# Attention and two MLPs in one kernel: transposed weights in one-bank buffers, sums in SBUF, gate after both products, another choice of engines

## The chip, the cores and the metric

The kernel runs on one core of a Trainium2 chip. The metric is the device time of one execution in microseconds (us). A core has TensorE (PE, matrix products, with a queue of weight loads shown as PEld), VectorE (DVE), ScalarE (ACT), GpSimd (POOL) and SyncE (SP, which here only issues transfers). PSUM, where PE writes, has eight banks, each of which holds 512 fp32 numbers per partition.

## The reference

```python
# q, k, v: 2 batches, 12 heads, 448 rows, 64 columns, fp32
scores = where(upper triangle, -1e9, q @ k.T / 8)
attn = exp(scores - rowmax);  attn = attn / (rowsum + 1e-9)
x = (attn @ v), heads side by side                    # 896 x 768
xn = x / sqrt(mean(x * x) + 1e-6) * rms_g
g = xn @ w_gate;  h = g * sigmoid(g) * (xn @ w_val)    # 768 -> 1536
x = h @ w_out                                         # 1536 -> 768
h = max(x @ moe2_w_in, 0);  out = (h * h) @ moe2_w_out # 768 -> 2048 -> 768
```

The MLP weights arrive as 64-bit floats, two 32-bit words each.

## The kernel before

Attention goes by pairs of heads: 2 batches with 6 pairs, 12 in all, each `step(p)`. Scores of a pair are written in two PSUM tiles of two banks (`s1`, `s2`, pool `ps_s`, two buffers: four banks). DVE takes row maxima (L368, L370), ACT turns them into biases (`nb`, L375) and computes exp with `accum_out` (L395), which leaves the row sums in `su`. `su` is a slice of one PSUM tile, `sums_`, a bank of its own that all pairs share (four slices in turn). DVE adds 1e-9 and inverts (L410, L411), and POOL multiplies the seven pieces of exponentials by the result (`ml`, L421). PE transposes them with an identity: `tr1` (L436) once per head for `p1`, and `tr2`, `tr3` (L442, L446) for `p2`, all into tiles of two banks from a pool with one buffer (`ps_t`). Four copies (`c_1` to `c_4`, by ACT or DVE through `copy`, L282) bring a pair's 2,048 columns into `pt`, and `values` (L485) multiplies them with v: four chunks for each of two heads, 16 matmuls into `o`. `finish` copies `o` to `xr`, and `square` and `add_square` (L507 to L512) sum squares for the normalisation. The last PSUM bank, `ps_o`, holds `o`.

Beside that, six weight tiles of the first MLP are made ready (`ahead_steps`): from the two words of each double come an exponent part (L179, L181), a sign (L187, L191), upper and lower bits (L195, L200), and a split into an upper part (L158) and a lower rest (L208). `norm` scales x of a batch (L567) and splits it the same way (L158, L160, L578). `ahead_products` then computes the first three column tiles of the first MLP for the first batch: 18 matmuls for the gate's product and 18 for the other (L647), in the two banks of one `ps_s` tile, with tanh (L658), the gate (L662) and the final product (`hh`, L669).

All of these steps go to one planner, `Order`. Each step has a due time, the engines that may do it with a duration each in us, the steps that it follows and the buffers that it takes. The planner repeatedly picks the step that can begin first, within SLACK by due time, and gives it the engine where begin + duration + COST is least. Steps are emitted in that order, so it fixes each engine's queue; on the chip each queue runs in order and waits for what it needs. `A_`, `D_`, `P_` and `E_` are the durations that the planner assumes for ACT, DVE, POOL and PE.

After the planned part, `mlp1` runs the same three column tiles for the second batch and then the remaining nine for both (`mm3`, L227 to L229), followed by the products with `w_out`, `moe2_w_in` and `moe2_w_out`. There the order is that of the program.

Of the kernel before, what the change touches and what calls it, by code (L numbers as in the profile page):

```python
# [8 lines left out]
F32 = mybir.dt.float32  # L9
# [9 lines left out]
P = 128  # L19
# [4 lines left out]
NF2 = DF2 // P  # L24
NPAIR = H // 2
WARM = 9
ACC = 0.16
CN = 112
NE = 3
STRIDE = 6.0  # L30
SLACK = 0.1
SWITCH = 0.18
COST = {"D": 0.6}
LAT = {"E": 0.3, "S": 0.0}


# [7 lines left out]
class Order:  # L44
# [9 lines left out]
    def add(self, due, opts, f, after=(), new=(), uses=(), mode=None, begin=0.0):  # L54

        t = dict(due=due, opts=opts, f=f, after=[a for a in after if a], new=new, uses=list(uses) + list(new),
                 mode=mode, begin=begin, end=None, eng=None, i=len(self.tasks))
        for b in t["uses"]:
            b.left += 1
        self.tasks.append(t)  # L60
        return t
# [55 lines left out]
def tile_attention_moe_moe2(ctx: ExitStack, tc: tile.TileContext, qk, v, wg, wv, wo, w2i, w2o, rms_g, out):  # L117
# [122 lines left out]
    at = att.enter_context(tc.tile_pool(name="at", bufs=2))  # L240
    atc = att.enter_context(tc.tile_pool(name="atc", bufs=1))
    ps_s = att.enter_context(tc.tile_pool(name="ps_s", bufs=2, space=PSUM))
    ps_t = att.enter_context(tc.tile_pool(name="ps_t", bufs=1, space=PSUM))
    ps_o = att.enter_context(tc.tile_pool(name="ps_o", bufs=1, space=PSUM))
    ps_n = att.enter_context(tc.tile_pool(name="ps_n", bufs=1, space=PSUM))
    sums_ = ps_n.tile([P, 512], F32, name="sums_")

    NPR = B * NPAIR
    SC = 1.0 / float(D) ** 0.5
# [20 lines left out]
    for i in range(2):  # L270
# [1 line left out]
        nc.gpsimd.memset(t[:, 1, S:], 0.0)  # L272
        p2t.append(t)
    L3 = 1408
    KO = (0, S, 896, 1344)

    order = Order(dict(qk=3, v=NV, s=2, p1=2, p2=2, t=1, pt=2, o=1, x=9, sq=1, ssq=1, rb=1, raw=2, wt=3, whl=3,
                       early=3, tt=2, tu=2, hh=2))
    BOTH = (slice(0, D), slice(D, P))

    def copy(e, o, i):
        (nc.scalar.copy if e == "A" else nc.vector.tensor_copy)(o, i)  # L282
# [5 lines left out]
        return 0.15 + n / 960  # L288

    def P_(n, two=False):  # L290
        return 0.14 + 0.0024 * n if two else 0.27 + 0.00108 * n

    def E_(n):
        return n / 600 + 0.05
# [7 lines left out]
    def step(p):  # L302
# [2 lines left out]
        T0 = p * STRIDE  # L305
        add = order.add
        bq, bv, b1, b2, bp1, bp2 = (order.buf(n) for n in ("qk", "v", "s", "s", "p1", "p2"))
        bt1, bt2, bpt, bo, bx = (order.buf(n) for n in ("t", "t", "pt", "o", "x"))

        def load_qk(e):  # L310
            z["qk"] = at.tile([P, 2, S], F32, tag="qk", name="qk", bufs=3)
# [47 lines left out]
        def mx(buf, o, n, k):  # L359
            def f(e):  # L360
                if k == 0:
                    z["mx"] = at.tile([P, 8], F32, tag="mx", name="mx", bufs=3)
                    z["nb"] = at.tile([P, 8], F32, tag="nb", name="nb", bufs=3)
                    z["su"] = sums_[:, 8 * (p % 4):8 * (p % 4 + 1)]
                    z["r"] = at.tile([P, 8], F32, tag="r", name="r", bufs=3)
                src = z[buf][:, :, o:o + n]
                if k == 6:
                    nc.vector.tensor_reduce(z["mx"][:, 6:7], src, mybir.AxisListType.XY, ALU.max)  # L368
                else:
                    nc.vector.tensor_reduce(z["mx"][:, k:k + 2], src, AX, ALU.max)  # L370
            return f
# [55 lines left out]
                           uses=[bp1 if k < 4 else bp2]))  # L427


        def tr1(h):  # L430
            def f(e):
                if h == 0:
                    z["t1"] = ps_t.tile([P, 2, 512], F32, tag="t", name="t1")
                for i, o in enumerate((0, 128, 256, 384)):

                    nc.tensor.transpose(z["t1"][:, h, o:o + P], z["p1"][:, h, o:o + P], ident)  # L436
            return f

        def tr2(e):
            z["t2"] = ps_t.tile([P, 2, 512], F32, tag="t", name="t2")  # L440
            for i in range(4):
                nc.tensor.transpose(z["t2"][:, 0, i * P:(i + 1) * P], z["p2"][:, 0, i * P:(i + 1) * P], ident)  # L442

        def tr3(e):
            for i in range(4):
                nc.tensor.transpose(z["t2"][:, 1, i * P:(i + 1) * P], z["p2"][:, 1, i * P:(i + 1) * P], ident)  # L446

        a1 = add(T0 + 7, {"E": 0.44}, tr1(0), [ml_[0], ml_[2]], new=[bt1], uses=[bp1], mode="f")
        a2 = add(T0 + 7, {"E": 0.44}, tr1(1), [ml_[1], ml_[3], a1], uses=[bt1, bp1], mode="f")
        a3 = add(T0 + 10, {"E": 0.44}, tr2, [ml_[4], ml_[5]], new=[bt2], uses=[bp2], mode="f")  # L450
        a4 = add(T0 + 10, {"E": 0.44}, tr3, [ml_[6], a3], uses=[bt2, bp2], mode="f")


        def c_1(e):
            z["pt"] = at.tile([P, 2, L3], F32, tag="pt", name="pt", bufs=2)
            copy(e, z["pt"][:, :, 0:128], z["t1"][:, :, 0:128])

        def c_2(e):
            copy(e, z["pt"][:, :, 256:256 + 3 * 320].rearrange("p h (k n) -> p h k n", n=320)[:, :, :, :128],
                 z["t1"][:, :, 128:].rearrange("p h (k n) -> p h k n", n=128))  # L460

        def c_3(e):

            copy(e, z["pt"][:, :, 128:128 + 2 * 320].rearrange("p h (k n) -> p h k n", n=320)[:, :, :, :128],
                 z["t2"][:, 0].rearrange("p (h k n) -> p h k n", h=2, n=128))

        def c_4(e):

            copy(e, z["pt"][:, :, 128:].rearrange("p h (k n) -> p h k n", n=320)[:, :, :, 256:],
                 z["t2"][:, 1].rearrange("p (k h n) -> p h k n", h=2, n=D))  # L470

        def c2opt(n):
            return {"A": A_(n), "D": D_(n)}

        y1 = add(T0 + 8, c2opt(256), c_1, [a1, a2], new=[bpt], uses=[bt1])
        y2 = add(T0 + 8, c2opt(768), c_2, [a1, a2, y1], uses=[bt1, bpt])
        y3 = add(T0 + 11, c2opt(512), c_3, [a3, y1], uses=[bt2, bpt])
        y4 = add(T0 + 11, c2opt(512), c_4, [a4, y1], uses=[bt2, bpt])

        def values(e):  # L480
            z["o"] = ps_o.tile([P, 512], F32, tag="o", name="o")
            for j in range(4):
                n = S - j * P
                for h in range(2):
                    nc.tensor.matmul(z["o"][BOTH[h], j * P:S], z["v"][:, j, h * D:(h + 1) * D],  # L485
                                     z["pt"][:, h, KO[j]:KO[j] + n], start=j == 0, stop=j == 3)

        va = add(T0 + 13, {"E": E_(1024) + 0.15}, values, [t_v, y1, y2, y3, y4], new=[bo], uses=[bpt, bv], mode="c")

        def finish(e):  # L490
            z["x"] = xrp.tile([P, S], F32, tag="xr", name="xr")
# [143 lines left out]
    def ahead_products(ft, due):  # L635

        z, add = {}, order.add
        bs, bt, bu, bh = order.buf("s"), order.buf("tt"), order.buf("tu"), order.buf("hh")
        last = None

        def products(k, i):
            def f(e):
                if k == 0 and i == 0:
                    z["ps"] = ps_s.tile([P, 2, 512], F32, tag="s", name="pgv")
                o, w, x = z["ps"][:, k, :S], ahead[2 * ft + k]["hl"], xs[0][i]
                for n, (a_, b_) in enumerate(((0, 0), (0, 1), (1, 0))):
                    nc.tensor.matmul(o, w[:, a_, i], x[:, b_], start=i == 0 and n == 0, stop=i == NCC - 1 and n == 2)  # L647
            return f

        for k in range(2):  # L650
            for i in range(NCC):
                new = [bs] if k == 0 and i == 0 else []
                last = add(due, {"E": 0.61}, products(k, i), [last, xl[0][i], ahead[2 * ft + k]["done"]],
                           new=new, uses=[ahead[2 * ft + k]["bw"]] + ([] if new else [bs]), mode="f")
            if k == 0:
                def f_tanh(e):
                    z["t"] = tmp.tile([P, S], F32, tag="t", name="t")
                    nc.scalar.activation(z["t"], z["ps"][:, 0, :S], AF.Tanh, scale=0.5)  # L658

                def f_gate(e):  # L660
                    z["w"] = tmp.tile([P, S], F32, tag="u", name="u")
                    nc.vector.scalar_tensor_tensor(z["w"], z["t"], 1.0, z["ps"][:, 0, :S], ALU.add, ALU.mult)  # L662

                g1 = add(due, {"A": A_(S)}, f_tanh, [last], new=[bt], uses=[bs])
                g2 = add(due, {"D": D_(S)}, f_gate, [g1], new=[bu], uses=[bs, bt])

        def f_hh(e):
            z["hh"] = tmp.tile([P, S], F32, tag="hh", name="hh")
            nc.vector.scalar_tensor_tensor(z["hh"], z["w"], 0.5, z["ps"][:, 1, :S], ALU.mult, ALU.mult)  # L669

        def f_hi(e):
            hs[0][ft] = slab(f"h0_{ft}", 0, ft)
            rnd(E(e), hs[0][ft][:, 0], z["hh"])

        def f_lo(e):
            E(e).tensor_sub(hs[0][ft][:, 1], z["hh"], hs[0][ft][:, 0].bitcast(F32))

        g3 = add(due, {"D": D_(S)}, f_hh, [g2, last], new=[bh], uses=[bs, bu])
        g4 = add(due, {"A": A_(S), "P": P_(S)}, f_hi, [g3], uses=[bh])
        add(due, {"P": P_(S, True), "D": D_(S)}, f_lo, [g4], uses=[bh])  # L680
# [120 lines left out]
```

## Time and profile before

| | us |
|---|---|
| median of three runs | 624.02 |
| lowest, highest | 622.49, 626.37 |
| the profiled execution | 624.11 |
| its span, from the first to the last instruction | 622.2 |

| engine | busy in the span |
|---|---|
| PE | 599.8 |
| PEld | 524.7 |
| DVE | 408.8 |
| POOL | 262.9 |
| ACT | 129.0 |

Busy times are averages over very different stretches: up to about 105 us all engines work on attention, the six weight tiles and the first normalisation; up to about 140 us PE finishes attention and the products that were taken ahead; from there to the end PE multiplies without a break. Matmuls are pipelined, so PE's busy time says that it had work and not that it worked at its peak. A wait is put down to whichever releaser came last.

### The profile page before, as it was taken

To read this page: it belongs to the slowest core of one execution; us is meant where nothing else is said; L and a number is where in the kernel's file an instruction comes from. 1 tells how busy PE (TensorE), PEld (TensorE's weight loads), DVE (VectorE), ACT (ScalarE), POOL (GpSimd) and SP (SyncE) were. 2 spreads that over 40 slices of the span, in tenths; PEclk is the share of its full clock that TensorE was granted. 3 is DMA by queue.
4 is the path that set the end of the run, shared out by engine and by line. 5 is a ranking of instruction groups with operands and counts; after the bars stand their busy time and mean duration, and the time that the engine had idled before them with its cause. 6 is when DMAs were issued, how large, how long until landed. Compare 5 with 4: busy or idle time off the path is not lost.

```text
span 622.2 us, 8412 instructions
## 1 busy us (share of the span) xinstructions
PE 599.8 (96%) x3269; PEld 524.7 (84%) x3269; DVE 408.8 (66%) x570; ACT 129.0 (21%) x341; POOL 262.9 (42%) x318
## 2 busy tenths in 40 slices
PE   7998888989999999999999999999999999999997
PEld 4665555869999999999999999999999999999996
DVE  3689798165888777777755555888888874544310
ACT  4886666331000000000010001111111100000000
POOL 4559899333433333333322222566554442222100
PEclk9999898998999999999999999999999999999999
DMA  6454521001524333333333333233333234433100
GB/s 162 140 150 173 186 72 61 2 1 55 176 80 146 114 117 121 108 102 101 111 124 121 102 102 103 101 102 102 106 108 103 82 117 158 131 104 133 44 29 31
DMA packets 19496, 65.04 MB, mean 105 GB/s; under 512 B 2048, under 2 KB 8960, under 8 KB 19456
## 3 DMA queue, kind: packets, MB, share of 16 engines
q1 hardware_dynamic: 19456, 64.50, 31.9%
q8 instruction: 26, 0.43, 0.3%
q14 instruction: 14, 0.11, 0.1%
HBM read 61.74 MB, written 2.75 MB: 104 GB/s over the span
## 4 chain that ended last, share of the span: by engine, by line
PE 87%; POOL 6%; DVE 3%; ACT 2%; issue 1%; DMA 1%; SPq 0%; POOLq 0%; ACTq 0%; DVEq 0%
PE py L228 17%; PE py L229 17%; PE py L227 17%; PE pg L227 4%; PE pg L228 4%; PE pg L229 4%; PE pv L228 4%; PE pv L229 4%; PE pv L227 4%; PE pgv L647 4%; POOL p2t L421 2%; PE s L334 2%; POOL p L421 2%; PE o L485 2%; DVE mx L370 1%
## 5 line engine op out<-in xcount | busy, mean ns | idle before, releaser
L158 POOL TENSOR_SCALAR whl<-wt 128x768 fp32r<-128x768 f32 (+1 forms) x70 | 65.9, 942 | 144.4 <-PE py L229 113.5
L208 DVE TENSOR_TENSOR whl<-wt,whl 128x768 fp32r<-128x768 f32 (+1 forms) x70 | 73.0, 1042 | 56.3 <-POOL whl L158 56.2
L181 POOL TENSOR_SCALAR wt<-wraw 128x768 f32<-128x768 f32 (+1 forms) x68 | 63.5, 935 | 53.6 <-DVE whl L208 48.0
L200 DVE SCALAR_TENSOR_TENSOR wt<-wraw,wt 128x768 uint32<-128x768 uint32 (+1 forms) x70 | 73.2, 1046 | 1.1
L227 PE MATMUL py<-y,whl 128*128 128x448 f32 x192 | 70.4, 367 | 0.0
L228 PE MATMUL py<-y,whl 128*128 128x448 f32 x192 | 70.4, 367 | 0.0
L229 PE MATMUL py<-y,whl 128*128 128x448 f32 x192 | 70.4, 366 | 0.0
L227 PE MATMUL py<-hh,whl 128*128 128x448 f32 x192 | 70.1, 365 | 0.0
L228 PE MATMUL py<-hh,whl 128*128 128x448 f32 x192 | 70.1, 365 | 0.0
L229 PE MATMUL py<-hh,whl 128*128 128x448 f32 x192 | 70.1, 365 | 0.0
L195 DVE SCALAR_TENSOR_TENSOR wt<-wt,wraw 128x768 uint32<-128x768 uint32 (+1 forms) x70 | 66.3, 947 | 2.1
L191 DVE TENSOR_SCALAR wraw<-wt 128x768 uint32<-128x768 uint32 (+1 forms) x66 | 37.2, 563 | 35.9 <-POOL wt L181 35.9
L158 POOL TENSOR_SCALAR hh<-hh 128x448 fp32r<-128x448 f32 x32 | 35.0, 1095 | 50.1 <-DVE hh L748 49.7
L227 PE MATMUL py<-h,whl 128*128 128x448 f32 x144 | 52.6, 365 | 0.0
L229 PE MATMUL py<-h,whl 128*128 128x448 f32 x144 | 52.6, 365 | 0.0
L228 PE MATMUL py<-h,whl 128*128 128x448 f32 x144 | 52.6, 365 | 0.0
L227 PE MATMUL pg<-x,whl 128*128 128x448 f32 x126 | 46.9, 372 | 0.7 <-DVE hh L669 0.7
L229 PE MATMUL pg<-x,whl 128*128 128x448 f32 x126 | 46.8, 371 | 0.0
L228 PE MATMUL pg<-x,whl 128*128 128x448 f32 x126 | 46.8, 371 | 0.0
L227 PE MATMUL pv<-x,whl 128*128 128x448 f32 x126 | 46.2, 367 | 0.0
L228 PE MATMUL pv<-x,whl 128*128 128x448 f32 x126 | 46.2, 367 | 0.0
L229 PE MATMUL pv<-x,whl 128*128 128x448 f32 x126 | 46.2, 367 | 0.0
(105 smaller groups left out, 1090.9 us busy)
## 6 DMA issues: line engine op xcount, KB each, us to landing
wraw<-in_w2i SPq DMA_DIRECT2D x16, 768.0 KB, 4.2
wraw<-in_wg SPq DMA_DIRECT2D x12, 768.0 KB, 4.4
wraw<-in_wv SPq DMA_DIRECT2D x12, 768.0 KB, 4.4
wraw<-in_wo SPq DMA_DIRECT2D x12, 768.0 KB, 4.3
wraw<-in_w2o SPq DMA_DIRECT2D x12, 640.0 KB, 4.2
qk<-in_qk SPq DMA_DIRECT2D x11, 448.0 KB, 4.6
wraw<-in_w2o SPq DMA_DIRECT2D x6, 768.0 KB, 4.4
out_t<-o SPq DMA_DIRECT2D x12, 224.0 KB, 1.9
```

What stands on the lines that cost most here:

```text
L158: eng.tensor_scalar(o, i, 1.0, 1.0, ALU.mult, ALU.mult)
L181: eng.tensor_scalar(e["t"], hi, 2.0 ** -112, 1.0, ALU.mult, ALU.mult)
L191: nc.vector.tensor_scalar(e["s"], e["t"].bitcast(U32), 0x80000000, None, ALU.bitwise_and)
L195: nc.vector.scalar_tensor_tensor(u, u, 3, e["s"], ALU.logical_shift_left, ALU.bitwise_or)
L200: nc.vector.scalar_tensor_tensor(u, lo, 29, u, ALU.logical_shift_right, ALU.bitwise_or)
L208: eng.tensor_sub(e["hl"][:, 1, :n], e["t"].rearrange("p (k n) -> p k n", n=P), e["hl"][:, 0, :n].bitcast(F32))
L227: nc.tensor.matmul(ps, w[:, 0, i], x[:, 0], start=first and i == 0, stop=False)
L228: nc.tensor.matmul(ps, w[:, 0, i], x[:, 1], start=False, stop=False)
L229: nc.tensor.matmul(ps, w[:, 1, i], x[:, 0], start=False, stop=last and i == n - 1)
L334: nc.tensor.matmul(s[:, h, o:o + n], z["qk"][BOTH[h], 0, qs], z["qk"][BOTH[h], 1, :n], start=True, stop=False)
L421: E(e).tensor_scalar(t, t, z["r"][:, k:k + 1], 1.0, ALU.mult, ALU.mult)
L647: nc.tensor.matmul(o, w[:, a_, i], x[:, b_], start=i == 0 and n == 0, stop=i == NCC - 1 and n == 2)
```

## The change

Transposes go through four steps `tr(k)` with a one-bank tile each, from a pool of three buffers; each has one copy `tc_(k)` of 512 columns. The layout of `pt` changes: the first chunk's transposed square lies at column 1216 (`K0`) and has matmuls of its own in `values`, which then has 18. `su` is a small SBUF tile for each pair in place of the PSUM bank. `f_tanh` and `f_gate` follow both products of a column tile, where they followed the first. The planner's constants change: ACT's surcharge for a sum is 0.2 in place of 0.16, its copies are 0.1 shorter, POOL's durations longer, DVE's COST 0.3 in place of 0.6, and POOL has a COST of 0.6 where it had none.

```diff
-ACC = 0.16
+ACC = 0.2
-COST = {"D": 0.6}
+COST = {"D": 0.3, "P": 0.6}
...
-    ps_t = att.enter_context(tc.tile_pool(name="ps_t", bufs=1, space=PSUM))
+    ps_t = att.enter_context(tc.tile_pool(name="ps_t", bufs=3, space=PSUM))
-    ps_n = att.enter_context(tc.tile_pool(name="ps_n", bufs=1, space=PSUM))
-    sums_ = ps_n.tile([P, 512], F32, name="sums_")
...
-    KO = (0, S, 896, 1344)
+    KO = (128, 448, 896, 1344)
+    K0 = 1216
...
     def P_(n, two=False):
-        return 0.14 + 0.0024 * n if two else 0.27 + 0.00108 * n
+        return 0.2 + 0.0025 * n if two else 0.32 + 0.00112 * n
...
-                    z["su"] = sums_[:, 8 * (p % 4):8 * (p % 4 + 1)]
+                    z["su"] = at.tile([P, 8], F32, tag="su", name="su", bufs=3)
...
+        def tr(k):
+            def f(e):
+                t = z["t", k] = ps_t.tile([P, 512], F32, tag="t", name="t")
+                src = z["p1"][:, k] if k < 2 else z["p2"][:, k - 2]
+                for i in range(4):
+                    o = (i + 1) % 4 if k < 2 else i
+                    nc.tensor.transpose(t[:, i * P:(i + 1) * P], src[:, o * P:(o + 1) * P], ident)
+            return f
...
+        for k in range(4):
+            bt = order.buf("t")
+            a_.append(add(T0 + (7 if k < 2 else 10), {"E": 0.44}, tr(k),
+                          [[ml_[0], ml_[2]], [ml_[1], ml_[3]], [ml_[4], ml_[5]], [ml_[6]]][k], new=[bt],
+                          uses=[bp1 if k < 2 else bp2], mode="f"))
+            y_.append(add(T0 + (8 if k < 2 else 11), {"A": A_(512) - 0.1, "D": D_(512)}, tc_(k), [a_[k]] + y_[:1],
+                          new=[bpt] if k == 0 else [], uses=[bt] + ([bpt] if k else [])))
 
         def c2opt(n):
-            return {"A": A_(n), "D": D_(n)}
+            return {"A": A_(n) - 0.1, "D": D_(n)}
...
             z["o"] = ps_o.tile([P, 512], F32, tag="o", name="o")
+            for h in range(2):
+                nc.tensor.matmul(z["o"][BOTH[h], :P], z["v"][:, 0, h * D:(h + 1) * D], z["pt"][:, h, K0:K0 + P],
+                                 start=True, stop=True)
             for j in range(4):
-                n = S - j * P
+                n = S - max(j, 1) * P
...
-            if k == 0:
-                def f_tanh(e):
...
+        g1 = add(due, {"A": A_(S)}, f_tanh, [last], new=[bt], uses=[bs])
+        g2 = add(due, {"D": D_(S)}, f_gate, [g1], new=[bu], uses=[bs, bt])
```

## Rows read from the trace of the kernel before

**Rows 1.** Busy time (and instructions) by stretch; then clock, DMA share, GB/s.
```profile
core 0: us, PE busy (x) PEld busy (x) DVE busy (x) ACT busy (x) POOL busy (x), PEclk, DMA share, GB/s
15.00:47.00 32.00, 30.71 (x292) 20.87 (x292) 23.19 (x50) 27.65 (x91) 18.93 (x32) 1.00 0.45 142
47.00:105.00 58.00, 48.28 (x403) 30.69 (x403) 51.96 (x84) 39.19 (x126) 55.07 (x67) 0.94 0.39 132
105.00:141.00 36.00, 32.21 (x174) 25.66 (x174) 16.05 (x26) 14.18 (x30) 14.86 (x17) 0.99 0.00 1
141.00:622.20 481.20, 477.40 (x2339) 440.14 (x2337) 311.90 (x395) 41.69 (x77) 168.20 (x182) 1.00 0.32 105
```

**Rows 2.** Waits, 47 to 105 us: total us, times, longest.
```profile
PE t L442 <- POOL p2t L421: 7.2, 6, 2.8
...
ACT p L395 <- DVE r L410: 5.3, 5, 1.7
...
DVE mx L370 <- PE s L338: 2.8, 3, 1.1
```

**Rows 3.** The chain that ended last, 47 to 105 us, by line.
```profile
by line: POOL p2t L421 18.7%; POOL p L421 17.5%; PE s L334 8.5%; issue 8.4%; POOL wt L181 5.7%; POOL wraw L187 5.7%; DVE mx L370 5.6%; PE t L446 5.3%; PE o L485 3.4%; POOL x L578 2.7%; DVE whl L208 2.2%; POOL x L158 2.1%; POOL ssq L512 1.9%
```

**Rows 4.** POOL's groups, 47 to 105 us: count, busy us, mean ns, idle before.
```profile
L187 POOL TENSOR_SCALAR wraw<-wt 128x768 f32<-128x768 f32 x4 | 5.3, 1329 | 0.4
L158 POOL TENSOR_SCALAR whl<-wt 128x768 fp32r<-128x768 f32 x6 | 5.0, 826 | 0.9 <-DVE wt L200 0.9
...
L181 POOL TENSOR_SCALAR wt<-wraw 128x768 f32<-128x768 f32 x4 | 4.3, 1072 | 0.0
L158 POOL TENSOR_SCALAR x<-xr 128x448 fp32r<-128x448 f32 x4 | 4.0, 1001 | 0.0
L578 POOL TENSOR_TENSOR x<-xr,x 128x448 fp32r<-128x448 f32 x3 | 4.0, 1334 | 0.1
L512 POOL TENSOR_TENSOR ssq<-ssq,sq 128x448 f32<-128x448 f32 x3 | 3.4, 1127 | 0.0
```

**Rows 5.** DVE's groups, 47 to 105 us.
```profile
L208 DVE TENSOR_TENSOR whl<-wt,whl 128x768 fp32r<-128x768 f32 x6 | 8.9, 1484 | 0.7 <-POOL whl L158 0.7
L200 DVE SCALAR_TENSOR_TENSOR wt<-wraw,wt 128x768 uint32<-128x768 uint32 x5 | 7.2, 1444 | 0.0
...
L282 DVE COPY xr<-o 128x448 f32<-128x448 f32 x5 | 3.0, 597 | 0.0
...
L512 DVE TENSOR_TENSOR ssq<-ssq,sq 128x448 f32<-128x448 f32 x2 | 1.7, 869 | 0.0
...
L191 DVE TENSOR_SCALAR wraw<-wt 128x768 uint32<-128x768 uint32 x1 | 0.5, 547 | 0.0
```

**Rows 6.** ACT's groups: sums and nb, 47 to 105 us; exponents, 0 to 140.
```profile
L395 ACT ACTIVATION_READ_ACCUMULATOR p<-s,nb 128x1 f32 x24 | 4.1, 170 | 0.0
...
L375 ACT ACTIVATE nb<-mx 128x3 f32<-128x3 f32 x6 | 1.2, 205 | 3.1 <-DVE mx L368 3.1
...
L179 ACT ACTIVATE wt<-wraw 128x768 f32<-128x768 f32 x2 | 1.9, 946 | 0.0
```

**Rows 7.** Two of DVE's groups, 150 to 500 us.
```profile
L200 DVE SCALAR_TENSOR_TENSOR wt<-wraw,wt 128x768 uint32<-128x768 uint32 x47 | 50.4, 1072 | 0.5
L208 DVE TENSOR_TENSOR whl<-wt,whl 128x768 fp32r<-128x768 f32 x47 | 49.4, 1051 | 16.5 <-POOL whl L158 16.4
```

**Rows 8.** Pieces of the chain in order of time: start, us, what.
```profile
33.56 1.88 PE o L485 x16
...
140.81 0.37 PE pg L228
```

**Rows 9.** PE's waits, 105 to 141 us: total us, times, longest.
```profile
PE pgv L647 <- DVE u L662: 1.6, 2, 0.8
PE pgv L647 <- ACT t L658: 1.3, 2, 0.6
PE pg L227 <- DVE hh L669: 0.7, 1, 0.7
```

**Rows 10.** The gate's group on DVE, 0 to 140 us.
```profile
L662 DVE SCALAR_TENSOR_TENSOR u<-t,pgv 128x448 f32<-128x448 f32 x3 | 1.9, 622 | 7.3 <-PE pgv L647 7.3
```

More of the change, by code (lines that the diff above doesn't have):

```diff
@@ L274, in tile_attention_moe_moe2 @@
     L3 = 1408
-    KO = (0, S, 896, 1344)
-    order = Order(dict(qk=3, v=NV, s=2, p1=2, p2=2, t=1, pt=2, o=1, x=9, sq=1, ssq=1, rb=1, raw=2, wt=3, whl=3,
+    KO = (128, 448, 896, 1344)
+    K0 = 1216
+    order = Order(dict(qk=3, v=NV, s=2, p1=2, p2=2, t=3, pt=2, o=1, x=9, sq=1, ssq=1, rb=1, raw=2, wt=3, whl=3,
                        early=3, tt=2, tu=2, hh=2))
@@ L307, in step @@
         bq, bv, b1, b2, bp1, bp2 = (order.buf(n) for n in ("qk", "v", "s", "s", "p1", "p2"))
-        bt1, bt2, bpt, bo, bx = (order.buf(n) for n in ("t", "t", "pt", "o", "x"))
+        bpt, bo, bx = (order.buf(n) for n in ("pt", "o", "x"))
         def load_qk(e):
@@ L427, in step @@
                            uses=[bp1 if k < 4 else bp2]))
-        def tr1(h):
+        def tr(k):
             def f(e):
[L432 to L436, printed above, removed]
-            return f
[L439 to L451, printed above, removed]
@@ L454, in c_1 @@
[L454 to L465, printed above, removed]
@@ L467, in c_4 @@
-        def c_4(e):
-            copy(e, z["pt"][:, :, 128:].rearrange("p h (k n) -> p h k n", n=320)[:, :, :, 256:],
-                 z["t2"][:, 1].rearrange("p (k h n) -> p h k n", h=2, n=D))
-        def c2opt(n):
-            return {"A": A_(n), "D": D_(n)}
[L475 to L478, printed above, removed]
+                t = z["t", k] = ps_t.tile([P, 512], F32, tag="t", name="t")
@@ new lines, in f, with tc_ @@
+                src = z["p1"][:, k] if k < 2 else z["p2"][:, k - 2]
+                for i in range(4):
+                    o = (i + 1) % 4 if k < 2 else i
+                    nc.tensor.transpose(t[:, i * P:(i + 1) * P], src[:, o * P:(o + 1) * P], ident)
+            return f
+        def tc_(k):
+            def f(e):
+                if "pt" not in z:
+                    z["pt"] = at.tile([P, 2, L3], F32, tag="pt", name="pt", bufs=2)
+                pt, t = z["pt"], z["t", k]
+                if k < 2:
+                    o = pt[:, k, 128:].rearrange("p (k n) -> p k n", n=320)[:, :, 128:256]
+                    t = t.rearrange("p (k n) -> p k n", n=P)
+                elif k == 2:
+                    o = pt[:, :, 128:768].rearrange("p h (k n) -> p h k n", n=320)[:, :, :, :P]
+                    t = t.rearrange("p (h k n) -> p h k n", h=2, n=P)
+                else:
+                    o = pt[:, :, 128:].rearrange("p h (k n) -> p h k n", n=320)[:, :, :, 256:]
+                    t = t.rearrange("p (k h n) -> p h k n", h=2, n=D)
+                copy(e, o, t)
+            return f
@@ new lines, in step @@
+        a_, y_ = [], []
+        for k in range(4):
[5 more added lines that the diff above has]
+                          new=[bpt] if k == 0 else [], uses=[bt] + ([bpt] if k else [])))
@@ L480, in values @@
+        def c2opt(n):
+            return {"A": A_(n) - 0.1, "D": D_(n)}
         def values(e):
             z["o"] = ps_o.tile([P, 512], F32, tag="o", name="o")
+            for h in range(2):
+                nc.tensor.matmul(z["o"][BOTH[h], :P], z["v"][:, 0, h * D:(h + 1) * D], z["pt"][:, h, K0:K0 + P],
+                                 start=True, stop=True)
             for j in range(4):
-                n = S - j * P
+                n = S - max(j, 1) * P
                 for h in range(2):
-                    nc.tensor.matmul(z["o"][BOTH[h], j * P:S], z["v"][:, j, h * D:(h + 1) * D],
+                    nc.tensor.matmul(z["o"][BOTH[h], S - n:S], z["v"][:, j, h * D:(h + 1) * D],
@@ L486, in values @@
                                      z["pt"][:, h, KO[j]:KO[j] + n], start=j == 0, stop=j == 3)
-        va = add(T0 + 13, {"E": E_(1024) + 0.15}, values, [t_v, y1, y2, y3, y4], new=[bo], uses=[bpt, bv], mode="c")
+        va = add(T0 + 13, {"E": E_(1024) + 0.2}, values, [t_v] + y_, new=[bo], uses=[bpt, bv], mode="c")
         def finish(e):
@@ L654, in ahead_products, with f_tanh, f_gate @@
                            new=new, uses=[ahead[2 * ft + k]["bw"]] + ([] if new else [bs]), mode="f")
-            if k == 0:
-                def f_tanh(e):
[L657 to L665, printed above, removed]
+        def f_tanh(e):
+            z["t"] = tmp.tile([P, S], F32, tag="t", name="t")
+            nc.scalar.activation(z["t"], z["ps"][:, 0, :S], AF.Tanh, scale=0.5)
+        def f_gate(e):
+            z["w"] = tmp.tile([P, S], F32, tag="u", name="u")
+            nc.vector.scalar_tensor_tensor(z["w"], z["t"], 1.0, z["ps"][:, 0, :S], ALU.add, ALU.mult)
+        g1 = add(due, {"A": A_(S)}, f_tanh, [last], new=[bt], uses=[bs])
+        g2 = add(due, {"D": D_(S)}, f_gate, [g1], new=[bu], uses=[bs, bt])
         def f_hh(e):
```

## Prediction

> **What bounds the kernel now.** I read the busy times by stretch first [rows 1]. They cut the execution in four. From 141 us to the end TensorE is busy for 477.4 of 481.2 us: it is the bound there, and nothing in the diff touches that code, so those 481 us stay. What the change can move is when this part begins. From 15 to 47 us, while attention runs almost alone, PE is busy for 30.7 of 32 us. From 47 to 105 us, where weight tiles and the first batch's normalisation run beside attention, PE is busy for only 48.3 of 58 us, POOL for 55.1, DVE for 52.0, ACT for 39.2. The mean granted clock of that stretch is 0.94, which is about 7 us at the lower of the two levels (1.2 of 2.4 GHz). From 105 to 141 us PE is the busy one again, with 3.8 us idle.
>
> The waits of the 58 us say who holds PE: the longest is 7.2 us for POOL's last step on the exponentials, p2t, ahead of their transposes [rows 2]. The chain of the same stretch confirms it: 36% is POOL's L421, and another 18%, 10.5 us, is POOL work that another engine could do (wt L181, wraw L187, x L578, x L158, ssq L512) [rows 3]. So POOL is the bound from 47 to 105 us, and DVE is next, at 90%.
>
> **POOL chosen less.** The planner takes, for each step, the engine with the least begin + duration + COST. With the numbers put into the line's formulas: a weight's sign (768 columns) was 1.10 on POOL against 1.30 on DVE and is now 1.78 against 1.00; the sum of squares was 1.215 against 1.217 and is now 1.92 against 0.92; an x's lower part was 1.21 against 1.60, now 1.92 against 1.30; exponents and upper parts of weights were 1.10 against 0.91 on ACT, now 1.78; an x's upper part 0.75 against 0.64, now 1.42. POOL now gets one only if the other engine comes free 0.6 to 1.0 later than it, and few steps in that plan last so long. In the 58 us these are 24 instructions and 26.0 us of POOL [rows 4]. On DVE the 4 signs would cost 0.55 each and the 3 sums 0.87, and the 3 lower parts, also two inputs of 448 columns, are taken at 0.87: 7.4 us [rows 5]. On ACT the other 14 are taken at the 0.95 of an exponent, which has the most columns of them: 13.3 us [rows 6]. I take two thirds to move: POOL 55.1 - 17.3 = 37.8, DVE 52.0 + 4.9 = 56.9, ACT 39.2 + 8.9 = 48.1.
>
> DVE then is the next to be late, and its price depends on POOL: L208 took 1.48 us here and 1.05 between 150 and 500 us, L200 1.44 and 1.07 [rows 5, 7]; POOL was busy for 95% of the first stretch and for 35% after 141 us [rows 1]. Six and five of them hold 2.6 + 1.9 = 4.5 us of such excess. At 65% POOL I give half back, 2.2. The Trainium skill, SBUF — State Buffer, section Who interferes with whom, says that a DVE instruction with two SBUF inputs and a GpSimd one that reads SBUF block each other for a whole instruction. Both lines are of that kind; if POOL's moved steps were the ones in the way, by that rule nearly all of the 4.5 would come back, for a sum some 2 us lower than mine.
>
> DVE is then 56.9 - 2.2 = 54.7. It also holds five copies of xr, 3.0 us, that ACT may do [rows 5]; I let three go there: 52.9, with ACT at 49.9, POOL at 38, PE at 48. DVE was idle for 6 us, 2.8 of them waiting for scores that PE wrote late because of POOL [rows 2]; this mostly ends. I take 53 for the 58 us: **-5.0**. The bounds: 0 (DVE full at 58), and PE's own need, 48.3 less the 3.5 us that 7 us at half the clock cost: 44.8, or -13.
>
> **Three one-bank transpose buffers, one copy each.** Four copies of 512 columns replace copies of 256, 768, 512 and 512: as many instructions and columns, so 0. Transposes may run ahead of the copies; what held PE was POOL, so 0 again, and the bound is the 1.3 us of idle PE between 15 and 47 us [rows 1]. The values product has 18 matmuls in place of 16, with the same 2,048 columns (448 becomes 128 + 320). The 16 take 1.88 us on the chain, 0.12 each [rows 8]. Two more cost between 0 (columns alone) and 0.24 per pair; since they bring no column I take a fifth: 0.05 x 12 = **+0.6** (bounds 0 and 2.8). PE is the bound from 15 to 47 us, so nothing hides it there.
>
> **Sums in SBUF.** All pairs' sums share one PSUM bank, and ACT's next exp waits for DVE's read of earlier sums: 5.3 us in five waits [rows 2]. That goes. Behind it on ACT stand exps and copies, then r on DVE, then POOL's L421; but POOL had a queue almost all the time, so I count **-0.5** (0 to -2). The write of a sum took 0.17 us; no row shows it into SBUF, the nearest being the small step nb, from SBUF into SBUF, at 0.205 [rows 6]. That bounds it at 0 to 0.035, 84 times: up to 2.9 us of ACT, hidden by ACT's 18.8 us idle in the 58; with ACT at 50 of 53 about half would count, 1.5. Nearer to the read that it still is than to nb, I take 0. The Trainium skill, ScalarE: Activation LUTs, section What happens when an exp ACTIVATE runs, says that ACT writes PSUM faster than SBUF, which speaks against this edit. By it the sum would be up to 1.5 us higher, and no run here shows it.
>
> **Both products, then the gate.** A column tile's two products lie in two banks of one tile. Before, PE stopped between them for tanh or for the gate: 2.9 us in four waits, and 0.7 for hh before the second batch starts [rows 9]. Now the gate of one tile runs under the next tile's 36 matmuls, 7.3 us at the 0.204 of the last stretch (477.4 over 2,339) [rows 1]. After the last tile nothing covers it: tanh, gate and product, each taken as the gate's 0.62 [rows 10] and 0.07 for its handover: 2.1 in place of 0.7. Net 2.1 - 0.7 - 2.9 = **-1.5** (bounds -2.9 if the bank is not waited for, +0.5 if the gate of one more tile stays bare). Next late would be the second batch's x, made by ACT, POOL and DVE in the same stretch; should it be as late as before, the 1.5 is lost, which lies inside these bounds. That batch's first ten matmuls ran at 0.37 [rows 8], the lower clock after those stops: 1.7 us that may go or stay; I leave it.
>
> **Sum.** -5.0 + 0.6 - 0.5 - 1.5 = -6.4. The profiled execution took 624.1 with a span of 622.2, against a median of 624.0, so from either base the time is 617.7.
>
> **The rivals.** *PE becomes the bound.* POOL's work moves and all is spread evenly; the stretch shrinks to between 44.8 and 48.3, say 46.5: -11.5 + 0.6 - 0.5 - 1.5, so 611. For it: PE idles for 9.7 us there. Against: with all 24 moved and the whole excess gone, POOL has 29.1, DVE 54.9 and ACT 52.5 us of work, 45.5 each only if perfectly spread. *DVE takes POOL's place.* All 7.4 us move, nothing goes to ACT: 52.0 + 7.4 - 2.2 = 57.2, a gain of 0.8, so 622. For it: DVE at 90%. *Slower: copies go to DVE as well.* D's COST falls from 0.6 to 0.3 and ACT's copy by 0.1, so that ACT loses a copy of 512 columns when it is free 0.39 later than DVE, where it was 0.59. If 8 of the 24 pt copies go, at the 0.60 of an xr copy [rows 5], DVE has 57.2 + 4.8 = 62, and with 3 us idle 65: +7 less 1.4, so 629.7. It decides once DVE has over 58 us of work for this stretch. Against: the planner sees DVE's own queue and sends steps elsewhere.
>
> **How the numbers follow.** Forecast (613 to 620) 0.44, PE-bound (607 to 613) 0.16, DVE in POOL's place (620 to 626) 0.25, slower (626 to 636) 0.15. About 1%, 6.2 us, is what a measurement of this kernel can tell from no change. Faster than 617.8 are the PE-bound case and some 0.7 of the forecast: 0.47. Over 630.2 lies most of the last: 0.12. The rest, 0.41, is within 1%. 608 to 627 leaves out the ends, under 0.2.
>
> **What would show it.** Right: POOL's busy time for the stretch down by 12 to 20 us; PE's wait on p2t under 4 us; no PE wait on u or t among the tile products, one of about 2 us before the second batch; no wait of an exp on r's read. Wrong: DVE without a gap before 105 us and scores unread (the DVE rivals), or POOL still full to 105 us, so that this part of the change does little.

## The result, and the profile after

The changed kernel takes 617.73 us (median of four runs, 616.47 to 619.41) where the kernel before took 623.78 beside it: a ratio of 0.990, with an interval of 0.986 to 0.9939. In a later group of runs it took 617.74 against 626.09, 0.9861 (0.9846 to 0.9875). The profiled execution took 617.8 with a span of 615.9. The forecast was 617.7.

Where the time went shows in the busy times by stretch. First the same stretches of the clock as in [rows 1]:

```profile
core 0: us, PE busy (x) PEld busy (x) DVE busy (x) ACT busy (x) POOL busy (x), PEclk, DMA share, GB/s
15.00:47.00 32.00, 31.38 (x319) 22.20 (x317) 24.86 (x51) 26.78 (x91) 19.58 (x35) 1.00 0.47 152
47.00:105.00 58.00, 48.48 (x451) 32.92 (x448) 56.42 (x95) 41.33 (x134) 51.17 (x62) 1.00 0.38 126
105.00:141.00 36.00, 33.84 (x169) 29.77 (x168) 17.06 (x27) 11.23 (x21) 9.70 (x10) 0.91 0.00 1
141.00:615.90 474.90, 471.49 (x2316) 434.70 (x2315) 309.66 (x395) 41.16 (x76) 167.23 (x179) 1.00 0.33 106
```

DVE has risen from 52.0 to 56.4 us of the 58 and POOL fallen from 55.1 to 51.2: DVE is the fullest engine now. The granted clock of this stretch rose from 0.94 to 1.00, and PE issued 451 matmuls where it issued 403. To compare equal work I cut by events: from pair 6's first scores to the last scores (called the stretch from here on), and from there to the second batch's first product (the tail). Before:

```profile
46.90:103.60 56.70, 47.77 (x399) 30.34 (x398) 50.63 (x84) 37.88 (x124) 53.77 (x65) 0.94 0.39 135
103.60:140.20 36.60, 32.07 (x176) 25.43 (x174) 17.45 (x28) 15.01 (x33) 16.12 (x18) 1.00 0.00 1
```

After:

```profile
45.70:97.30 51.60, 44.65 (x424) 30.01 (x424) 50.12 (x84) 37.97 (x124) 46.41 (x58) 1.00 0.40 131
97.30:134.30 37.00, 32.30 (x182) 27.43 (x182) 23.05 (x38) 14.69 (x34) 15.68 (x16) 0.95 0.06 22
```

So 1.2 us were saved ahead of pair 6, 5.1 in the attention stretch, and 0.4 were lost in the tail; the second batch starts 5.9 us earlier. After it the two executions differ by 0.4. Part of the 5.1 is the clock, which stood at 0.94 before and at 1.00 after. A second profile of the changed kernel has 0.94 in this stretch, as the kernel before had:

```profile
45.65:98.56 52.91, 47.11 (x424) 31.53 (x423) 49.52 (x84) 37.86 (x124) 46.53 (x58) 0.94 0.40 130
```

At an equal clock the stretch gained 3.8 us. The tail of that profile, with no lower clock in it, took 35.6 us, 1.0 less than before; stretch and tail together are as long as in the first profile within 0.2 us.

The waits of the stretch from 47 to 105 us answer to [rows 2] (total us, times, longest):

```profile
PE t L436 <- POOL p L420: 4.9, 6, 1.8
...
PE o L472 <- issue: 1.7, 1, 1.7
...
PE ssqc L524 <- DVE ssq L504: 1.6, 1, 1.6
...
PE t L436 <- POOL p2t L420: 0.8, 4, 0.3
```

The wait on p2t fell from 7.2 to 0.8 us; one on p, the first half of a pair, came in its place. In the stretch cut by events, PE's waits for POOL fell from 7.5 to 3.1 us in all. ACT's wait for r's read is gone from the list. The chain by line, from 40 to 97.3 us, is now headed by DVE:

```profile
by line: DVE mx L369 11.7%; POOL p L420 10.5%; DVE r L409 6.4%; PE s L333 6.2%; PE t L436 6.1%; issue 6.1%; DVE wt L195 5.5%; DVE ssq L504 5.4%; POOL p2t L420 4.8%; DVE whl L208 4.5%; DVE xr L559 4.0%; DVE xr L281 3.8%; DVE mx L367 3.7%; DV
```

POOL's optional steps there, against [rows 4] (count, busy us, mean ns, idle before):

```profile
L181 POOL TENSOR_SCALAR wt<-wraw 128x768 f32<-128x768 f32 x4 | 4.7, 1175 | 0.0
...
L158 POOL TENSOR_SCALAR whl<-wt 128x768 fp32r<-128x768 f32 x5 | 4.1, 827 | 1.3 <-DVE wt L200 1.3
L187 POOL TENSOR_SCALAR wraw<-wt 128x768 f32<-128x768 f32 x2 | 2.4, 1185 | 0.2
L158 POOL TENSOR_SCALAR x<-xr 128x448 fp32r<-128x448 f32 x3 | 2.0, 681 | 0.0
L570 POOL TENSOR_TENSOR x<-xr,x 128x448 fp32r<-128x448 f32 x1 | 1.4, 1380 | 0.1
```

They are 15 in place of 24, and 14.6 us in place of 26.0. DVE's groups, against [rows 5], show a relief and a new cost:

```profile
L208 DVE TENSOR_TENSOR whl<-wt,whl 128x768 fp32r<-128x768 f32 x6 | 6.5, 1082 | 0.0
L200 DVE SCALAR_TENSOR_TENSOR wt<-wraw,wt 128x768 uint32<-128x768 uint32 x6 | 5.8, 972 | 0.0
...
L409 DVE TENSOR_SCALAR r<-su 128x4 f32<-128x4 f32 x6 | 3.5, 586 | 0.0
L409 DVE TENSOR_SCALAR r<-su 128x3 f32<-128x3 f32 x7 | 3.4, 491 | 0.0
```

L208 went from 1.48 to 1.08 and L200 from 1.44 to 0.97. L409, the tiny addition that reads the sums, took 0.15 when the sums lay in PSUM and takes 0.5 to 0.6 here, 6.9 us in all. One case in order of time shows why (start, us), POOL first and then DVE:

```profile
72.25 0.83 POOL L158 TENSOR_SCALAR whl<-wt 128x768 fp32r<-128x768 f32 x1
73.48 0.91 POOL L420 TENSOR_SCALAR p<-p,r 128x128 f32<-128x128 f32 x1 [0.40 <-DVE r L410]
```

```profile
72.38 0.73 DVE L409 TENSOR_SCALAR r<-su 128x4 f32<-128x4 f32 x1
73.14 0.18 DVE L410 RECIPROCAL r<-r 128x4 f32<-128x4 f32 x1
```

DVE's step of four columns began 0.13 us after POOL's and ended 0.03 us after it. POOL then waited 0.40 us for the reciprocal behind it. The other cases are alike: of the 24 such steps in this trace, twelve lasted 0.155 to 0.169 us and twelve 0.195 to 1.094, and each of the longer ones ended 0.02 to 0.03 us after an instruction of POOL that had begun before it.

### The profile page after: what moved, and what is told of

The parts are those of the page before. It is cut to its first block, busy times and chain, and to the rows that moved or that the text cites. A ratio compares the mean times of both kernels' runs of the same rounds, so it can differ in the third digit from the quotient of the medians.

```text
span 615.9 us, 8498 instructions
## 1 busy us (share of the span) xinstructions
PE 596.1 (97%) x3317; PEld 527.1 (86%) x3317; DVE 414.0 (67%) x581; ACT 126.8 (21%) x341; POOL 253.8 (41%) x307
## 4 chain that ended last, share of the span: by engine, by line
PE 89%; DVE 6%; POOL 2%; issue 1%; DMA 1%; ACT 0%; SPq 0%; POOLq 0%; ACTq 0%; DVEq 0%
PE py L227 17%; PE py L228 17%; PE py L229 17%; PE pg L227 4%; PE pg L228 4%; PE pg L229 4%; PE pv L228 4%; PE pv L227 4%; PE pv L229 4%; PE pgv L639 4%; PE s L333 2%; PE t L436 2%; POOL p L420 2%; DVE mx L369 1%; PE o L477 1%; PE s L346 1%
## 5 line engine op out<-in xcount | busy, mean ns | idle before, releaser
L208 DVE TENSOR_TENSOR whl<-wt,whl 128x768 fp32r<-128x768 f32 (+1 forms) x70 | 70.5, 1007 | 56.7 <-POOL whl L158 56.5
L181 POOL TENSOR_SCALAR wt<-wraw 128x768 f32<-128x768 f32 (+1 forms) x70 | 67.0, 958 | 52.8 <-DVE whl L208 47.6
L200 DVE SCALAR_TENSOR_TENSOR wt<-wraw,wt 128x768 uint32<-128x768 uint32 (+1 forms) x70 | 70.9, 1012 | 1.1
```

Of the source, the lines that this page charges most:

```text
L181: eng.tensor_scalar(e["t"], hi, 2.0 ** -112, 1.0, ALU.mult, ALU.mult)
L200: nc.vector.scalar_tensor_tensor(u, lo, 29, u, ALU.logical_shift_right, ALU.bitwise_or)
L208: eng.tensor_sub(e["hl"][:, 1, :n], e["t"].rearrange("p (k n) -> p k n", n=P), e["hl"][:, 0, :n].bitcast(F32))
```

## The experiments

The question was which part carries the gain, since the forecast gave nearly all of it to the choice of engines. Each ratio is to the kernel before on the same chip; it is the recorded one, with its interval, and can differ from the quotient of the two medians beside it. The changed kernel stands at 0.9861 and 0.990 on this scale.

**Sums in SBUF alone** (in the kernel before, same order of steps):

```diff
-                    z["su"] = sums_[:, 8 * (p % 4):8 * (p % 4 + 1)]
+                    z["su"] = at.tile([P, 8], F32, tag="su", name="su", bufs=3)
```

> The kernel before with one edit: each pair's sums in a small SBUF tile instead of the shared PSUM bank; the order of all steps is that of before. Theory (prediction): ACT's 6 us of waits for r's read vanish but POOL had its queue, so the time is 623 to 624.5. In the trace of the changed kernel r's read of the sums takes 0.40 us on average where it took 0.15, because it now stands behind POOL's instruction; with POOL busier in this order the mean should be at or over 0.4. Rival A: the ACT waits were on the path, 618 to 621. Rival B: the slower read, ahead of each of POOL's multiplications, costs more than the waits gave, 625 to 628.

Measured: 626.94 against 624.03; 1.0022 (0.9994 to 1.0051). No gain, and rather a loss: rival B, at the edge of what this measurement can tell. ACT's waits for r's read are gone, and L410, r's read in this kernel, has a mean of 0.33 us from 15 to 140 us, where it had 0.15; not the 0.4 expected. The stretch from pair 6's to the last scores:

```profile
46.18:105.80 59.62, 50.19 (x400) 30.47 (x400) 54.91 (x82) 37.92 (x126) 53.40 (x65) 0.91 0.38 127
```

59.6 us, against 56.7, with 0.91 of the clock against 0.94; POOL is without work for 6.2 of them, against 2.9.

**The same without the addition:**

```diff
-                nc.vector.tensor_scalar(z["r"][:, a:b], z["su"][:, a:b], 1.0e-9, 1.0, ALU.add, ALU.mult)
-                nc.vector.reciprocal(z["r"][:, a:b], z["r"][:, a:b])
+                nc.vector.reciprocal(z["r"][:, a:b], z["su"][:, a:b])
```

> As s_only (the order of before, sums in SBUF), but the reciprocal reads the sums directly; the addition of 1e-9 is left out (a sum is at least 1, since the row's largest exponential is 1). Theory (found in s_only): the sums in SBUF lost 2.9 us because the addition's read from SBUF stood behind POOL's instruction (0.33 in place of 0.15 on average, on the way to each of POOL's multiplications). With it gone and ACT's waits gone too, the time is 621 to 624. Rival: the loss came from the slower write of the sums on ACT (0.21 in place of 0.17), which stays: 626 to 627.

Measured: 625.05 against 625.80; 0.9986 (0.9959 to 1.0013). The loss is gone within the error, but it is no faster than before: in the old order, ACT's 5.3 us of waits [rows 2] were worth less than 1 us by the ratio, and at most 2.6 by its interval. The stretch is as long as with the addition:

```profile
46.15:106.20 60.05, 52.42 (x400) 32.19 (x399) 50.45 (x71) 38.04 (x126) 54.20 (x66) 0.86 0.36 126
```

So leaving the addition out doesn't bring the stretch back to the 56.7 us of before. The granted clock is lower still, 0.86, and POOL waits for r for 5.4 us, as with the sums alone (5.8). Whether the clock or this wait comes first is not shown.

**The changed kernel without the addition:**

> The changed kernel with the addition of 1e-9 left out, so that only the reciprocal reads the sums; the order is that of the changed kernel. The addition has 9.5 us of DVE there, 24 times 0.40. Theory: DVE is the bound from 47 to 105 us and the read sits in front of POOL's multiplications, so 2 to 4 us come back: 614 to 616. Rival: something else holds that stretch and the reciprocal is as long: 617 to 618.

Measured: 615.24 (612.74 to 616.75), 0.9835 (0.9781 to 0.9889), 2.5 us under the changed kernel's median. The interval meets the changed kernel's. On the same chip, a run that differs from the changed kernel only in spare banks (below) took 618.25 (617.23 to 619.19), more in each of its executions than any of these. The one reciprocal that is left costs as much as ever, so what reads SBUF on DVE is not slow as such; that particular form was:

```profile
L409 DVE RECIPROCAL r<-su 128x4 f32<-128x4 f32 (+1 forms) x22 | 3.6, 165 | 0.0
```

The stretch, however, hardly shows it:

```profile
44.65:95.70 51.05, 44.59 (x424) 29.99 (x423) 46.72 (x74) 37.96 (x125) 47.99 (x57) 1.00 0.43 137
```

DVE has 3.4 us less work in it than in the changed kernel, and the stretch is 0.5 shorter. Another 1.0 came ahead of pair 6, and the tail took 35.2 us, against 37.0 and 35.6 in the two profiles of the changed kernel. So DVE, though the fullest engine, does not set the pace alone either.

**The planner's constants alone**, without the copies' 0.1, in the kernel before:

```diff
-ACC = 0.16
-COST = {"D": 0.6}
+ACC = 0.2
+COST = {"D": 0.3, "P": 0.6}
...
-        return 0.14 + 0.0024 * n if two else 0.27 + 0.00108 * n
+        return 0.2 + 0.0025 * n if two else 0.32 + 0.00112 * n
```

> The kernel before with the planner's new ACC, COST and POOL durations alone. Theory (prediction): the stretch of pairs 6 to 11 shrinks by about 5 us, so 618 to 620, and POOL's optional steps there fall from 24 to about 15. Rival: without the three buffers and the SBUF sums the moved work only makes DVE the bound, 622 to 627.

Measured: 621.44 against 624.03; 0.9938 (0.9911 to 0.9965). Faster, by 2.6 us in the medians and 3.9 by the ratio, whose interval (2.2 to 5.6) still holds the 5 of the theory; but in the trace not where it said:

```profile
48.53:105.30 56.77, 49.15 (x399) 30.92 (x398) 48.73 (x89) 38.69 (x121) 45.05 (x57) 0.91 0.38 132
```

POOL has 8.7 us less work in this stretch than before, and DVE has 1.9 less too, and yet the stretch is as long: 56.8 us. Two things stand against this single trace: the clock in the stretch is 0.91, against 0.94 before, and the profiled execution was the slowest of ten, 623.6 us. Where the others gained, no trace shows. POOL's waits in it:

```profile
POOL p L421 <- DVE r L411: 5.2, 6, 1.3
POOL p2t L421 <- DVE r L411: 5.2, 2, 2.8
```

POOL now idles for 10.4 us because a pair's reciprocals are not there yet: relieved of work, it waits for the step ahead of it in the chain.

**The changed kernel with the old constants** (the same lines the other way round; the copies' 0.1 stays):

> The changed kernel with the planner's ACC, COST and POOL durations of before (the copies' 0.1 stays): buffers, SBUF sums and the later gate remain. Theory (prediction): the stretch from pair 6's scores to the last scores goes back from 51.6 to about 56.7 us because POOL takes its 24 steps again, so 622 to 624. Rival: the finer buffers and the sums carried the gain there, 617 to 619.

Measured: 619.12 against 624.03; 0.9892 (0.984 to 0.9943). The trace and the time answer differently:

```profile
46.05:102.10 56.05, 46.34 (x423) 30.59 (x422) 52.27 (x79) 39.44 (x128) 52.31 (x61) 0.97 0.40 131
```

The stretch is back at 56.1 us, as the theory said, but the time is not back at 622 to 624, since the tail is shorter: 35.1 us (102.1 to 137.2) against 37.0, and no lower clock follows it. The interval holds the changed kernel's 0.9861 and 0.990, so the time itself doesn't tell the two apart.

**Buffers and sums alone**, first with the copies' 0.1 and then without any new constant. To the changed kernel with the old constants this brings back the gate between the products:

```diff
+            if k == 0:
+                def f_tanh(e):
...
+                g1 = add(due, {"A": A_(S)}, f_tanh, [last], new=[bt], uses=[bs])
+                g2 = add(due, {"D": D_(S)}, f_gate, [g1], new=[bu], uses=[bs, bt])
```

> The changed kernel with the planner's old ACC, COST and POOL durations and with the gate again after the first product: only the three one-bank buffers, the SBUF sums and copies 0.1 cheaper remain. The kernel before with SBUF sums alone took 626.9. Theory (prediction): the buffers are worth nothing, so 625 to 628. Rival: since old_consts, which also has the later gate, took 619.1, the buffers carry most of that: 620 to 622.

Measured: 621.91 against 625.80; 0.9947 (0.9924 to 0.9971). The stretch:

```profile
47.74:102.70 54.96, 45.13 (x423) 29.80 (x422) 52.44 (x79) 39.23 (x128) 52.52 (x61) 1.00 0.42 134
```

From the run above this one differs only by the gate, and both have the full clock in the tail: 36.9 us here (102.7 to 139.55), 35.1 there. So the later gate is worth 1.8 us in the tail.

```diff
-            y_.append(add(T0 + (8 if k < 2 else 11), {"A": A_(512) - 0.1, "D": D_(512)}, tc_(k), [a_[k]] + y_[:1],
+            y_.append(add(T0 + (8 if k < 2 else 11), {"A": A_(512), "D": D_(512)}, tc_(k), [a_[k]] + y_[:1],
...
-            return {"A": A_(n) - 0.1, "D": D_(n)}
+            return {"A": A_(n), "D": D_(n)}
```

> st_old with the copies' 0.1 taken back too: of the change only the three one-bank buffers with their four copies and the SBUF sums remain, and all planner constants are those of before. s_only (sums alone) was 1.0022 of before and st_old 0.9947. Theory: the gain of 0.75% is the buffers' finer grain, so 0.993 to 0.997 of before. Rival: it was the cheaper copies, that is where the planner puts them, and the buffers are worth nothing as the prediction had it: 1.000 to 1.004.

Measured: 623.05 against 626.69; 0.9934 (0.9912 to 0.9956). The interval does not meet that of the sums alone (0.9994 to 1.0051): the buffers, with the one copy each and the order that follows, gain 0.9% by the ratios, some 5.5 us; the medians, both taken on one chip, differ by 3.9. The cheaper copies do not carry it. The stretch:

```profile
46.40:103.30 56.90, 45.83 (x423) 30.00 (x422) 51.87 (x82) 37.50 (x123) 55.66 (x64) 1.00 0.40 134
```

It is 2.7 us shorter than with the sums alone, at a clock of 1.00 against 0.91, and no shorter than the 56.7 of the kernel before at 0.94. POOL, which had no work for 6.2 us, is now idle for 1.2: it is the bound almost without a gap. The chain of this stretch, by line, says the same, with 53% on POOL's multiplications:

```profile
by line: POOL p L420 33.8%; POOL p2t L420 19.1%; issue 12.1%; POOL ssq L504 5.1%; DVE wt L195 4.8%; POOL wt L181 3.2%; POOL whl L158 3.0%; DVE r L409 2.7%; PE t L436 2.4%; POOL x L158 1.9%; DVE mx L367 1.9%; POOL wraw L187 1.6%; DVE wraw L1
```

**Two buffers in place of three** (`bufs=2`, `t=2`), in the changed kernel:

> The changed kernel with two one-bank transpose buffers instead of three, which is the PSUM space of before in finer pieces; the planner knows of two. st_old, with buffers and sums alone, was 0.75% faster than s_only, with sums alone. Theory: it is the finer grain (a buffer is free after one copy of 512 columns, not after two copies of 1,024) that helps, so 617 to 619 as with three. Rival: it is the third bank, which lets transposes run ahead: 621 to 623. The prediction's step (buffers worth nothing) also expects 617 to 619.

Measured: 618.10 against 626.09; 0.987 (0.9853 to 0.9887), beside 0.9861 for the changed kernel on the same chip. The third bank, which the move of the sums set free, is not what helps.

**The gate back between the products**, in the changed kernel:

> The changed kernel with tanh and gate again after the first product of a column tile. Theory (prediction): four stops of PE of 2.9 us in all come back and the last wait falls from 2.2 to 0.7, so 1.5 us slower, 619 to 620. Rival: in the changed kernel other work stands between the products of the first two tiles, so that only the last tile's 1.4 us of stops return and the end saves 1.5: no difference, 617 to 618.

Measured: 620.23 against 624.03; 0.9894 (0.9847 to 0.9942), 2.5 us over the changed kernel's median, though the interval holds the changed kernel's ratios. PE's waits from 100 to 139 us:

```profile
PE t L436 <- POOL p L420: 2.6, 2, 1.8
PE pgv L639 <- ACT t L650: 2.0, 3, 0.7
PE pg L227 <- DVE hh L661: 1.5, 1, 1.5
```

Against 2.6 and 2.2 in the changed kernel, 1.3 us more. The early pairs of the profiled run had a stretch at the lower clock, so that pair 6 began 1.6 us later, and its total doesn't measure this edit. The tail does, beside the second profile of the changed kernel: 38.2 us against 35.6, both at the full clock. In the changed kernel the lower clock follows the wait and takes 1.6 us back after the tail, so that 1.0 is left.

**The changed kernel again**, beside the run with two buffers and the last one below:

> The changed kernel itself, on one chip with the other runs of this group. All theories: 0.99 of before, 616.5 to 619.5; the profile tells how much of a single trace is the lower clock at the start and at the second batch's beginning (up to 1.7 us at either place).

Measured: 617.74 (616.38 to 617.99), 0.9861 (0.9846 to 0.9875).

**The end of the products taken ahead.** Other banks for the second batch:

```diff
     ps_m = ctx.enter_context(tc.tile_pool(name="ps_m", bufs=8, space=PSUM))
+    for _ in range(2):
+        ps_m.tile([P, 512], F32, tag="m", name="skip")
```

> The changed kernel with the second batch's first products in other banks than the last column tile's, so that PE need not wait for that tile's tanh, gate and product. Theory: PE's wait of 2.2 us goes, and perhaps the 1.7 us at the lower clock behind it: 614 to 616. Rival: the second batch's x, whose lower parts end close to that point, holds PE instead: 617 to 618.

Measured: 618.25 against 625.80; 0.9887 (0.9837 to 0.9937): nothing. The wait is unchanged, and on the same step, so neither theory holds: it is not the bank, and not the second batch's x:

```profile
133.79 0.44 PE L227 MATMUL pg<-x,whl 128*128 128x448 f32 x1 [2.17 <-DVE hh L661]
```

What is left is that the pool of the scores is closed at that point, so that the new pool's first tile may wait for the closed pool's last reader. So the pool was kept open, and the MLP given the other four banks; the addition of 1e-9 was left out as well:

```diff
-    ps_s = att.enter_context(tc.tile_pool(name="ps_s", bufs=2, space=PSUM))
+    ps_s = ctx.enter_context(tc.tile_pool(name="ps_s", bufs=2, space=PSUM))
...
-    ps_m = ctx.enter_context(tc.tile_pool(name="ps_m", bufs=8, space=PSUM))
+    ps_m = ctx.enter_context(tc.tile_pool(name="ps_m", bufs=4, space=PSUM))
```

> no_add, with the scores' PSUM pool kept open, so that the second batch's first products lie in the four banks of the transposes and of o. skip_banks still waited 2.2 us for the last tile's product, so it is the closing of the pool that waits and not a bank. Theory: without the closing PE goes on at once, 2 us less than no_add's 615.2, and up to 1.7 less if the lower clock behind the wait goes too: 611 to 613.5. Rival: the second batch's x comes last, or four banks are too few for the rest: 615 or more.

Measured: 611.92 (610.91 to 613.20) against 626.09; 0.9777 (0.976 to 0.9793). It beats both kernels, by 5.8 us the changed one on the same chip, of which the missing addition has some 2.5. PE goes from one product to the next, and at the full clock:

```profile
118.66 10.27 PE L638 MATMUL pgv<-x,whl 128*128 128x448 f32 x48
128.77 0.37 PE L227 MATMUL pg<-x,whl 128*128 128x448 f32 x1
128.97 0.37 PE L228 MATMUL pg<-x,whl 128*128 128x448 f32 x1
```

The products start 0.20 us apart; in the changed kernel nine of them started 0.37 apart after the wait. So the wait went when the pool stayed open. The new tiles lie in other banks here too, those of the transposes and of `o`, so this run alone doesn't separate the two; skip_banks, where other banks left the wait as it was, speaks for the closing.

## Why the prediction came out, and what in it was wrong

**The sum** was right to 0.1 us in the median, which was luck in part: errors of several us in its terms cancelled, and the runs themselves scatter by 3 us.

**POOL chosen less, -5.0.** The stretch did lose 5.1 us, 3.8 of them at an equal clock, DVE did become the fullest engine, and PE's waits for POOL did fall, from 7.5 to 3.1 us. But the step that gave all of this to the choice of engines failed. With the constants alone POOL's load fell by 8.7 us and the stretch stayed at 56.8; with the new buffers and the old constants it was 55.0 to 56.9 in three traces; only with both was it 51.6 and 52.9. (The times alone don't show such an interplay: 0.6% for the constants and 0.7% for sums and buffers add up to the changed kernel's 1.0 to 1.4%.) The steps that moved were also fewer than two thirds: 11.4 us of POOL's time left, not 17.3, and POOL kept 51 us of the 58 where I had 38, partly because a multiplication took 0.80 us on average where it had taken 0.72 (36.9 us for 46, against 30.2 for 42). So the sign that the prediction named, 12 to 20 us less for POOL, did not appear: it was 3.9 in the 58 us and 7.4 in the stretch cut by events. What appeared, DVE almost without a gap, is nearer to the sign of its DVE rivals. Over the whole kernel, taking the constants back cost 1.4 us in the medians, which the interval doesn't tell from nothing, as the tail gave the rest back.

**Three one-bank buffers, 0.** This was the mistake, and the other half of the first one. I argued that PE never waited for a copy, and bounded the gain by the 1.3 us of idle PE in the early stretch. The runs show 0.9% against the sums alone, and 0.7% against the kernel before. How they gain it is in part open. One reading is that they take the gaps out of POOL's queue. With the sums alone POOL idled for 6.2 us of the stretch, with the constants alone for 11.7, 10.4 of them waiting for r; with the new buffers and the old constants for 1.2. By it, less work for POOL shortens the stretch only where r is ready sooner. The prediction had seen POOL full in the kernel before and concluded that its load alone set the pace. But the kernel before had gaps of no more than 2.9 us, and old_consts, with the new buffers, has 3.7, so this reading is not shown. Nor did any run have the new constants with the sums alone, so the buffers' part in it is not isolated. That the finer buffers act through the order that the planner can then write, and not through a wait that vanished, is inferred: no wait for a copy was there to vanish, and the third bank is not needed.

The clock is part of it, and here no small one. In the ten runs with the sums alone the granted clock of the whole execution was 0.982 to 0.992, in the four with the buffers too 0.991 to 1.000 (on average 0.989 and 0.995). What that is worth can be seen in the kernel before, whose 19 runs on the same chip had 0.997 in five, at 623.5 us on average, and 0.982 to 0.989 in eight, at 627.4. By that proportion, an estimate, some 2 us of the buffers' gain go with the clock; whether the finer buffers cause the higher clock is not shown. In the stretch alone it is less: two profiles of the changed kernel, at 1.00 and at 0.94, took 51.6 and 52.9 us, so 0.06 of it cost 1.3 us there. The 3.5 us that I had in the bound for it were too many.

**Two matmuls more, +0.6.** The count was wrong: the trace records each of these matmuls twice, so that the 16 of before are 8 in the code, and two new ones in the code bring them to 20, and not to 18. Even four more cost nothing: the values take 0.37 + 1.52 = 1.89 us on the chain after, against 1.88 [rows 8], and undisturbed pairs follow each other in 6.90 us as before (6.91). Columns set the price here, as the row per column should have told me.

**Sums in SBUF, -0.5.** As it stands the edit gained nothing and rather lost. ACT's waits went, as said, and were worth next to nothing, as nearly said. The bound for the write nearly held, while the 0 that I took did not: 0.17 became 0.21, against nb's 0.205.

```profile
L394 ACT ACTIVATION_READ_ACCUMULATOR p<-s,nb 128x1 f32 x24 | 4.9, 206 | 0.0
L394 ACT ACTIVATION_READ_ACCUMULATOR p2t<-s,nb 128x1 f32 x21 | 4.4, 211 | 0.0
```

The direction is the one of the Trainium skill's page ScalarE: Activation LUTs that the prediction cited (it stands in the section Step-by-step: what each stage is for), and the trace agrees: 0.04 us each, 3.2 us of ACT for 84 of them. No run shows them on the path. What I did not list is the other end, DVE's read of the same tile: 5.3 us more of DVE in the 58 us (6.9 against some 1.6), and ahead of POOL's multiplications. Taking the addition out gave 2.5 us, though only 0.5 of it in the stretch. The Trainium skill, SBUF — State Buffer, section Who interferes with whom, names it: a copy or tensor_scalar of DVE can take the port pair that it shares with GpSimd, and then one waits for the other's whole instruction. The twelve longer steps above agree, and from PSUM the same step never took over 0.17.

**DVE's price.** I gave back half of 4.5 us for L208 and L200. At 1.08 and 0.97 they gave back more, (1.48 - 1.08) x 6 + (1.44 - 0.97) x 5 = 4.8, though POOL was still busy for 88% of the 58 us. So the share of POOL's busy time, on which I scaled, was not the measure: in st_pure, with POOL busy for 98% of the 58 us, L208 took 1.55 but L200 0.98. The rule of the Trainium skill that the prediction cited here, by which nearly all comes back, was nearer. L409 then took the gain away.

**Both products, then the gate, -1.5.** Right, with its parts, and 1.8 us in the tail where two runs differ in it alone: PE's stops for tanh and gate, 2.9 us, are gone, and the wait before the second batch is 2.2 where 0.7 was [rows 9]:

```profile
PE t L436 <- POOL p L420: 2.6, 2, 1.8
PE pg L227 <- DVE hh L661: 2.2, 1, 2.2
```

Net 1.4. What the prediction missed is the first of these lines, a wait in the same tail that does not come from the gate: the last pair's four multiplications took 4.43 us beside DVE's work on x and weights, PE waited 2.6 us, and the fifteen products behind it took 4.49 us instead of 3.1, partly at the lower clock. That is why the tail of this execution is 0.4 us longer and not 1.5 shorter; in the second profile, with the same two waits but without the lower clock, it is 1.0 shorter. And the wait at its end did not go with another bank, which the prediction named, but where the pool was kept open.

## What to carry to other kernels

Less work for the engine that looks like the bound helps only if the next thing in its chain is ready sooner: look for what it would wait for once it is free, try the two edits together and each alone, and compare traces at an equal granted clock. When a tile moves from PSUM to SBUF, price its reader too: a step of four columns on DVE cost up to 1.09 us once it read SBUF beside a busy POOL. And a sum of several edits that comes out right proves none of its terms: the constants, priced here at 5 us, gave 2.6 alone in the medians (3.9 by the ratio), and in the one trace of them nothing in their own stretch.

## What the runs showed of the hardware

DVE's tensor_scalar of three or four fp32 columns from SBUF lasted 0.155 to 1.094 us in the changed kernel's first trace, each of the twelve over 0.17 ending within 0.03 us of an instruction of POOL, while the reciprocal of the same columns, from the same SBUF tile, had a mean of 0.165 in no_add. Reading out exp's accumulator took 0.17 us into PSUM and 0.21 into SBUF. And one program, profiled twice, had 1.00 and 0.94 of the clock in the same stretch, at 51.6 and 52.9 us.
